# Two parts of P times V in the two banks of one tile, maxima passes six steps ahead, and outputs ahead of a new down pair: an attention and GEGLU kernel

## The chip, the cores and the metric

The kernel runs on one core of a Trainium2 chip. The metric is device microseconds (us) of one execution, the median over several runs; lower is better. The profile comes from one further execution that the hardware profiler recorded. PE is the matrix engine (TensorE), PEld its weight loads, DVE is VectorE, ACT is ScalarE, POOL is GpSimd, SP is the engine that issues most DMAs.

## The reference

A layer norm of x (2048 rows of 576) feeds two branches, and the result joins them. `wqkv`, `wo` and the three GEGLU weights are random; every product below is computed to float32 accuracy, which the kernel reaches by splitting operands into a high and a low float16 half and adding up three products.

```python
def _A_ref(x, wqkv, wo):            # S = 2048, D = 576, H = 32, Dh = 18
    qkv = (lambda x, *d: x.transpose(*d))((x @ wqkv).reshape(B, S, 3, H, Dh), 2, 0, 3, 1, 4)
    q, k, v = qkv[0], qkv[1], qkv[2]
    scores = jnp.einsum("bhqd,bhkd->bhqk", q, k) * (Dh ** -0.5)
    p = _softmax(scores, axis=-1)
    o = jnp.einsum("bhqk,bhkd->bhqd", p, v)
    return (lambda x, *d: x.transpose(*d))(o, 0, 2, 1, 3).reshape(B, S, D) @ wo
def _B_ref(x, w_gate, w_up, w_down):            # 576 -> 4608 -> 576
    h = _gelu(jnp.einsum("bsd,df->bsf", x, w_gate)) * jnp.einsum("bsd,df->bsf", x, w_up)
    return jnp.einsum("bsf,fd->bsd", h, w_down)
xn = _layernorm(x, axis=-1)
return x + _A_ref(xn, wqkv, wo) * _silu(_B_ref(xn, w_gate, w_up, w_down))
```

## The kernel before

**The work and its order.** The 32 heads go in 16 pairs. A main loop runs over the pairs p and, in each, over 64 steps i (lines 1696 to 1807). A step takes one block of scores of the pair, 128 keys by 512 queries for both heads (`qk2`, matmuls at L1402), turns it into exponentials P on ACT (L1408, or two calls L1410 and L1411 where the heads have different scales), and adds one block of an earlier pass over the scores of a later pair (`qk1`, matmuls at L1348), of which DVE takes the row maxima (L1351). Steps 0 to 31 are one half of the pair's queries, steps 32 to 63 the other. Between these stand the matmuls of the GEGLU branch: slots of gate and up products (`g_run`, matmuls at L496), down stages (`DownPair.run`, L758), and in the last pair slots of the output product with `wo` (`out_run`, L939). All of a core's PE instructions go in one order, fixed when the program is built; a planner (`make_plan`) spreads slots and stages over the steps by estimated costs, and `subtick` lets queued work of the other engines (loading and splitting weights, norms) into their own orders.

**P times V.** Every two steps give one unit (one block of 128 keys for a half's queries), and units wait in `pend`. `flush` takes them out and calls `burst`: for each unit eight passes on PE (four matmuls of float32, two passes each, 4 at a time side by side, L1427) add into one PSUM bank, and DVE then copies (L1433, at a half's start) or adds (L1435) that bank into the sum `osb`. A burst covers units of one half only. Where `pend` holds the end of one half and the start of the next, `flush` makes two parts of it, each with its own tile and its own add.

**PSUM.** `s1` and `s2` have two banks each for scores. `ma` and `mb` have one bank each; gate and up slots write them, and ACT empties them at the end of a unit of slots (L661 for gate into `gs`, L672 for up into `gv`; early in the run L542 and DVE L547 for the rest of q and k). `md` is a tile of two banks: a pair of down stages writes both and DVE adds them to `y` (L778). `MTile` (line 182) hands out `ma`, `mb` and `md` in program order, and a writer waits by semaphore until the tile's readers are through. A burst of one part takes `md`. A burst of two parts takes `ma` for the first and `md` for the second, or `ma` and `mb` where a down stage stands in that step and holds `md`.

**Maxima.** The passes `qk1` run AHEAD = 8 steps ahead of their pair: step i of pair p does block i + 8 of pair p + 1 or, from step 56, block i - 56 of pair p + 2. `max_end` closes a pair's maxima in three moves, at steps 55, 58 and 61: a last reduce on DVE (L1363) and three POOL operations (L1364 to L1366), a transpose on DVE (L1370) with a write to memory by SP (L1372), and two reads by SP (L1377) that put the maxima as two more rows into `QT`, from which the first `qk2` of that pair reads them. Queries and keys of pair p + 2 are loaded by SP at step 44 (`load_qk`). Ahead of the main loop, a prologue loop runs AHEAD + 1 steps of one `qk1` of pair 1 and 14 slots of gate and up.

**The last pair.** There is no gate and up stream any more. A step of the last pair does a down stage if one is open or can be opened, and then slots of the output product (L939), which `OutPair` puts into `ma` and `mb` or, when wide, into `md`; DVE (L979, L972) empties them into `ob`.

Of the kernel before, what the change touches and what calls it, by code (L numbers as in the profile page):

```python
# [12 lines left out]
F32 = mybir.dt.float32  # L13
# [3 lines left out]
ALU = mybir.AluOpType  # L17
# [3 lines left out]
P = 128  # L21
NT = S // P
NB = S // 512
NPAIR = H // 2
# [70 lines left out]
def kernel(ctx: ExitStack, tc: tile.TileContext, x, wqkv, wo, w_gate, w_up, w_down, out):  # L95
    nc = tc.nc
# [78 lines left out]
    def until(cond):  # L175
        while not cond():
            assert defer.items or bg
            subtick()
# [911 lines left out]
    def use(tag):  # L1090
        blocks[0] += 1
        return tag
# [226 lines left out]
            subtick()  # L1319


    AHEAD = 8
    QT, KT, VT, PM = {}, {}, {}, {}

    def load_qk(p):
# [17 lines left out]
    def qk1(p, item):  # L1343
        qt, kb = divmod(item, 4)
        s1 = ps.tile([P, 2, 512], F32, tag=use(("s1", "s2")[item % 2 if p == 0 or item < AHEAD and p == 1 else 0]), name=f"s1_{p}_{item}")
        for h in range(2):
# [67 lines left out]
    final_norm = deque()  # L1414
    osum = {}

    def burst(todo, tag):

        p, qh, k0, _, _ = todo[0]
        k1 = todo[-1][2]  # L1420
        t = MTile(tag, [P, 512], F32, 1)
        for _, _, kt, pa, pb in todo:
            for b, pt in enumerate((pa, pb)):
                for h in range(2):
                    qd = 64 * b + 32 * h
                    c0 = 38 * kt + 19 * h
                    nc.tensor.matmul(  # L1427
                        t.t[qd:qd + 32, :], VT[p][:, c0:c0 + 32], pt[:, h],
                        start=kt == k0, stop=kt == k1, skip_group_check=True,
                    )  # L1430
        if k0 == 0:
            osum[p, qh] = ap.tile([P, 512], F32, tag="osb", name=f"osb_{p}_{qh}", bufs=2)
            nc.vector.tensor_copy(osum[p, qh], t.t)  # L1433
        else:
            nc.vector.tensor_tensor(osum[p, qh], t.t, osum[p, qh], op=ALU.add)  # L1435
        t.done()
        if k1 == NT - 1:
            norm(p, qh)
# [119 lines left out]
    items = iter(range(64))  # L1558
    for k in range(AHEAD + 1):
        if k in (0, 2, 4):  # L1560
# [8 lines left out]
    pend = []  # L1569
    dn = None  # L1570
# [79 lines left out]

    def flush(tags):

        for tag in tags:
            if not pend:
                return
            n = next((k + 1 for k, u in enumerate(pend) if u[2] == NT - 1), len(pend))
            burst(pend[:n], tag)
            del pend[:n]

    units = deque([*range(8, NT), *range(8)])  # L1660
    tail = W()
# [33 lines left out]
    for p in range(NPAIR):  # L1695
        if p not in VT:
            load_v(p)
        more = p + 1 < NPAIR
        for i in range(4 * NT):
            s, half = divmod(i, 2)  # L1700
            qh, kt = divmod(s, NT)
            if p == NPAIR - 2:
                qh = 1 - qh
            if i == 0:
                until(lambda: mdone.get(p))
            if i == 44 and p + 2 < NPAIR:
                load_qk(p + 2)
            kp = p + 1 if i < 64 - AHEAD else p + 2
            if i == 64 - AHEAD:
                items = iter(range(64))  # L1710
            pt = qk2(p, 2 * qh + half, kt, "s2" if more else ("s1", "s2")[i % 2])
            if half == 0:
                pa = pt
            else:
                pend.append((p, qh, kt, pa, pt))
            if kp < NPAIR:
                qk1(kp, next(items))
            if i == 61 and more:
                steps[2]()
            now = 64 * p + i  # L1720
            held = 2 * len(pend) + (half == 0)
            if not more and i == 32:
                tail.keep = KEEP_END
            if gs.left == 0 and gs.pair is None and not gs.closed and not plan:
                load_ohl(OUT_ORDER[0])
                u = tail.unit
                late = False
                d = dn is not None or (
                    len(dnq) > 1 and held < 5 and (u is None or not u.wide)
                )  # L1730
                if d:
                    if dn is None:
                        dn = DownPair()
                    late = dn.run()
                run = pend and dn is None and (held >= 6 or kt == NT - 1 and half == 1 and i < 63)
                run = run or held >= 8
                subtick(dict(FREE, T=2.0) if not more else {"A": 0.75, "V": 0.75, "T": 2.0})
                if late:
                    dn.evac()
                    dn = None  # L1740
                if run:
                    wide = u.wide if u is not None else not tail.wide
                    flush(("ma", "mb") if dn is not None or wide else ("md", "md"))
                else:
                    if gq and i % 2:
                        for fn in gq.popleft():
                            fn()
                    if final_norm:
                        final_norm.popleft()()
                    if d or more:  # L1750
                        out_run(5 if d else 10)
                    else:
                        n = 28 * max(0, len(units) - tail.keep) + (28 if tail.unit is not None else 0)
                        credit = min(credit + min(9, n / (0.75 * (32 - i % 32))), 18)
                        while credit >= 4:
                            u = tail.unit
                            r = 14 if u is None else (u.slots - u.k) or 14
                            n = r if r <= 10 or credit >= r else (r + 1) // 2
                            n0 = tail.slots
                            out_run(n)  # L1760
                            credit -= tail.slots - n0
                            if tail.unit is not None or tail.slots == n0:
                                break
            else:
                if not plan and gs.pair is None and not gs.closed:
                    plan.extend(make_plan(now, held, dn is not None, len(dnq) // 2))
                step = plan.popleft() if plan else None
                late = False
                if step is None:
                    d = dn is not None or len(dnq) > 1 and held < 6  # L1770
                else:
                    d = step[0]
                behind = d and summed and not gs.closed
                summed = False
                if d:
                    dleft[0] -= 1
                if d and not behind:
                    if dn is None:
                        dn = DownPair()
                    late = dn.run()  # L1780
                if gs.closed:
                    gs.closed = False
                    if late:
                        dn.evac()
                        dn = None
                    subtick({"A": 2.2, "V": 0.8 if late else 2.2 if now < 256 else 1.5, "T": 0.7 + 0.86 * len(pend) + 0.73 * d}, 6)
                    two = any(u[2] == NT - 1 for u in pend[:-1])
                    flush(("ma", "mb") if d else ("ma", "md") if two else ("md", "ma"))
                    summed = not d
                else:  # L1790
                    quick = late or step is not None and step[2] < 1.45 and len(bg) < 70
                    subtick({
                        "A": 0.75, "V": 0.25 if quick else 0.75,
                        "T": 2.0 if step is None else 0.45 + step[2],
                    })
                    if late:
                        dn.evac()
                        dn = None
                    g_run(7 if step is None else step[1] or 0)
                    if behind:  # L1800
                        dn = DownPair()
                        dn.run()
            if more and i == 58:
                steps[1]()
            if more and i == 55:
                steps = max_end(p + 1)
                steps[0]()
    assert dn is None
# [5 lines left out]
        final_norm.popleft()()  # L1814
    u = tail.unit
    wide = u.wide if u is not None else not tail.wide
    flush(("ma", "mb") if wide else ("md", "md"))
    tail.keep = 0

    while final_norm:  # L1820
# [8 lines left out]
    for st in units:  # L1829
        u = OutPair(st, tail.wide)  # L1830
# [5 lines left out]
    for k, u in enumerate(stages):  # L1836
        sums = final_out(k) if k < 4 else None
# [38 lines left out]
```

## Time and profile before

| | |
|---|---|
| median of 3 runs | 2566.24 us (2565.88 to 2567.41) |
| the profiled execution | 2566.02 us, of which the span of the trace is 2563.9 us |
| PE busy, share of the span | 2494.2 us, 97% |
| DVE | 1843.1 us, 72% |
| ACT | 1657.5 us, 65% |
| POOL | 1550.5 us, 60% |
| mean granted clock of PE | 0.996 |

The execution's own time is 2.1 us longer than the span of its trace. In the rows of the profile, an instruction's group reads: line, engine, operation, output tile and input tiles, shape, count, then busy time, the mean of one in ns, and the idle time before it with what ended it. In a timeline, the first number is the start in us, the second how long the group of equal instructions lasted from the first start to the last end, and square brackets give the idle time ahead of it and what released it.

### The profile page before, as it was taken

To read this page: it belongs to the slowest core of one execution; us is meant where nothing else is said; L and a number is where in the kernel's file an instruction comes from. 1 tells how busy PE (TensorE), PEld (TensorE's weight loads), DVE (VectorE), ACT (ScalarE), POOL (GpSimd) and SP (SyncE) were. 2 spreads that over 40 slices of the span, in tenths; PEclk is the share of its full clock that TensorE was granted. 3 is DMA by queue.
4 is the path that set the end of the run, shared out by engine and by line. 5 is a ranking of instruction groups with operands and counts; after the bars stand their busy time and mean duration, and the time that the engine had idled before them with its cause. 6 is when DMAs were issued, how large, how long until landed. Compare 5 with 4: busy or idle time off the path is not lost.

```text
span 2563.9 us, 60635 instructions
## 1 busy us (share of the span) xinstructions
PE 2494.2 (97%) x25800; PEld 1314.3 (51%) x25800; DVE 1843.1 (72%) x2114; ACT 1657.5 (65%) x2066; POOL 1550.5 (60%) x1593
## 2 busy tenths in 40 slices
PE   7898999999999999999999999999999999999998
PEld 6554445455554545445454454555555545545555
DVE  7676778777776778777777777776777767677534
ACT  6125666766767666767666666677766666666664
POOL 4347664666638554758667676757576676757513
PEclk9999999999999999999999999999999999999999
DMA  4430112101130012201020111101011101100124
GB/s 154 134 103 13 31 39 80 38 19 52 31 86 20 24 41 65 46 23 52 14 52 11 38 30 40 51 15 52 16 34 30 40 22 41 45 13 14 38 63 139
DMA packets 139686, 118.66 MB, mean 46 GB/s; under 512 B 64810, under 2 KB 118832, under 8 KB 139417
## 3 DMA queue, kind: packets, MB, share of 16 engines
q1 hardware_dynamic: 136553, 106.92, 15.5%
q8 instruction: 203, 3.33, 0.6%
q0 software_dynamic: 1568, 5.37, 0.6%
q10 hardware_dynamic: 1296, 2.51, 0.3%
q14 instruction: 66, 0.54, 0.1%
HBM read 84.89 MB, written 29.61 MB: 45 GB/s over the span
## 4 chain that ended last, share of the span: by engine, by line
PE 85%; DVE 5%; ACT 3%; DMA 3%; POOL 2%; issue 2%; SPq 1%; ACTq 0%; POOLq 0%; DVEq 0%
PE mb_t L496 17%; PE ma_t L496 16%; PE md_t L758 16%; PE md_t L1427 12%; PE s L1402 9%; PE s L1348 8%; PE ma_t L1427 5%; DVE PM L1351 2%; ACT P L1408 1%; PE md_t L939 1%; DMA mxd_j<-mx_j 1%; PE pv_t L515 1%; ACT gs L661 1%; PE mb_t L1427 0%; PE mc_t L515 0%
## 5 line engine op out<-in xcount | busy, mean ns | idle before, releaser
L1351 DVE TENSOR_REDUCE PM<-s 128x2 f32<-128x1024 f32 x1024 | 1250.6, 1224 | 397.3 <-PE s L1348 387.0
L1408 ACT ACTIVATE P<-s,etab 128x1024 f32<-128x1024 f32 x896 | 996.0, 1113 | 600.9 <-PE s L1402 594.1
L496 PE MATMUL ma_t<-XHT,whi_c 64*128 64x512 f16 x1440 | 542.2, 377 | 7.6 <-ACT gs L661 3.9
L496 PE MATMUL mb_t<-XHT,whi_c 64*128 64x512 f16 x1440 | 542.1, 376 | 2.8 <-ACT gv L672 2.5
L496 PE MATMUL ma_t<-XHT,wlo_c 64*128 64x512 f16 x1296 | 487.7, 376 | 0.0
L496 PE MATMUL mb_t<-XHT,wlo_c 64*128 64x512 f16 x1152 | 433.6, 376 | 0.0
L496 PE MATMUL ma_t<-XL,whi_c 64*128 64x512 f16 x1152 | 433.5, 376 | 0.0
L496 PE MATMUL mb_t<-XL,whi_c 64*128 64x512 f16 x1152 | 433.4, 376 | 0.0
L1402 PE MATMUL s<-QT,KT 56*128 56x512 f16 x2048 | 408.4, 379 | 4.1 <-DVE PM L1351 1.3
L1348 PE MATMUL s<-KT,QT 54*128 54x512 f16 x2048 | 401.6, 377 | 5.2 <-DVE PM L1351 3.0
L496 PEld LDWEIGHTS <-whi_c 64*128 64x128 f16 x5184 | 279.2, 94 | 245.3 <-issue 23.1
L758 PE MATMUL md_t<-dhi_c,hhi 64*128 64x288 f16 x2304 | 349.3, 283 | 2.0 <-DVE y L778 1.2
L758 PE MATMUL md_t<-dhi_c,hlo 64*128 64x288 f16 x2304 | 349.0, 282 | 0.0
L758 PE MATMUL md_t<-dlo_c,hhi 64*128 64x288 f16 x2304 | 348.5, 282 | 0.0
L1427 PE MATMUL md_t<-P,VT 128*32 128x512 f32 x2872 | 334.4, 596 | 0.0
L758 PEld LDWEIGHTS <-hhi 64*128 64x128 f16 x4608 | 251.5, 94 | 136.2 <-issue 15.0
L697 POOL TENSOR_SCALAR tw<-tw 128x512 f32<-128x512 f32 x144 | 90.7, 630 | 317.4 <-ACT tw L690 316.3
L719 POOL TENSOR_TENSOR hlo<-gv,hhi 128x512 f16<-128x512 f32 x144 | 167.6, 1164 | 186.6 <-ACT hhi L712 182.8
L1402 PEld LDWEIGHTS <-KT 56*128 56x128 f16 x2048 | 124.9, 94 | 237.4 <-issue 153.4
L684 POOL TENSOR_TENSOR tw<-gs 128x512 f32<-128x512 f32 x144 | 150.8, 1047 | 145.7 <-ACT gs L661 145.2
L778 DVE SCALAR_TENSOR_TENSOR y<-md_t,c_c,y 128x576 f32<-128x576 f32 x272 | 219.2, 806 | 15.7 <-PE md_t L758 15.6
L496 PEld LDWEIGHTS <-wlo_c 64*128 64x128 f16 x2592 | 141.8, 94 | 118.0 <-issue 1.3
(264 smaller groups left out, 3943.6 us busy)
## 6 DMA issues: line engine op xcount, KB each, us to landing
draw_c<-in_B_w_down SPq DMA_DIRECT2D x18, 576.0 KB
raw_c<-in_B_w_gate SPq DMA_DIRECT2D x18, 512.0 KB
raw_c<-in_B_w_up SPq DMA_DIRECT2D x18, 512.0 KB
obr<-rd SPq DMA_DIRECT2D x30, 256.0 KB
KT<-KD SPq DMA_DIRECT2D x32, 224.0 KB
QT<-QD SPq DMA_DIRECT2D x32, 216.0 KB
VS<-vst POOLq DMA_DIRECT2D x16, 304.0 KB, 2.6
VT<-VS SPq DMA_DIRECT2D x16, 304.0 KB
```

Source lines behind the costliest of these rows:

```text
L496: m = nc.tensor.matmul(o, lw, xx, start=self.stage == 0 and self.k == 0, stop=self.stage == 1 and self.k == self.slots - 1, skip_group_che ...
L515: nc.tensor.matmul(o, xx(t), ww[:, t, i, :], start=(k == 0), stop=False)
L684: gp.tensor_tensor(st["t"], st["g"], st["g"], op=ALU.mult)
L697: gp.tensor_scalar(st["t"], st["t"], 1.0, 1.0, op0=ALU.mult, op1=ALU.add)
L719: gp.tensor_tensor(hs.lo[:, ft], st["v"], hs.hi[:, ft], op=ALU.subtract)
L758: m = nc.tensor.matmul(self.t.t[:, hf, 0:288], a[r, ft, sl], b[r, ft, 288 * hf:288 * hf + 288], start=self.stage == 0 and k == 0, stop=sel ...
L778: nc.vector.scalar_tensor_tensor(yy, y, w.c, yy, op0=ALU.mult, op1=ALU.add)
L1348: nc.tensor.matmul(s1[:, h], QT[p][r, P * qt:P * qt + P], KT[p][r, 512 * kb:512 * kb + 512], start=True, stop=True)
L1351: nc.vector.tensor_reduce(PM[p][:, :, qt, kb:kb + 1], s1, op=ALU.max, axis=AX.X)
L1402: nc.tensor.matmul(s2[:, h], KT[p][r, P * kt:P * kt + P], QT[p][r, 512 * qb:512 * qb + 512], start=True, stop=True)
L1408: nc.scalar.activation(pt, s2, AF.Exp, scale=ETAB[j0])
L1427: nc.tensor.matmul(t.t[qd:qd + 32, :], VT[p][:, c0:c0 + 32], pt[:, h], start=kt == k0, stop=kt == k1, skip_group_check=True,)
```

## The change

Three edits. (1) AHEAD goes from 8 to 6, and with it the places of the three moves of `max_end` (steps 57, 60, 62 in place of 55, 58, 61) and of `load_qk` (step 48 in place of 44). The prologue runs 7 steps in place of 9. (2) Where a burst has two parts and no down stage stands in the step, both parts go into the two banks of one `md` tile, each with its own add; it was `ma` and `md`. A burst of one part still takes `md`. (3) In the last pair, in a step in which a down pair is opened, its first stage comes behind the slots of the output product instead of ahead of them.

```diff
-    AHEAD = 8
+    AHEAD = 6
-    def burst(todo, tag):
+    def burst(todo, tag, both=None, bank=0):
-        t = MTile(tag, [P, 512], F32, 1)
+        t = MTile(tag, [P, 512], F32, 1) if both is None else both
+        sums = t.t if both is None else t.t[:, bank]
...
-                        t.t[qd:qd + 32, :], VT[p][:, c0:c0 + 32], pt[:, h],
+                        sums[qd:qd + 32, :], VT[p][:, c0:c0 + 32], pt[:, h],
...
-            nc.vector.tensor_tensor(osum[p, qh], t.t, osum[p, qh], op=ALU.add)
+            nc.vector.tensor_tensor(osum[p, qh], sums, osum[p, qh], op=ALU.add)
...
     def flush(tags):
-        for tag in tags:
-            if not pend:
-                return
+        parts = []
+        while pend:
             n = next((k + 1 for k, u in enumerate(pend) if u[2] == NT - 1), len(pend))
-            burst(pend[:n], tag)
+            parts.append(pend[:n])
             del pend[:n]
+        if len(parts) == 2 and "md" in tags:
+            both = MTile("md", [P, 2, 512], F32, 2)
+            for bank, part in enumerate(parts):
+                burst(part, "md", both, bank)
+        else:
+            for part, tag in zip(parts, tags):
+                burst(part, tag)
...
-            if i == 44 and p + 2 < NPAIR:
+            if i == 48 and p + 2 < NPAIR:
...
-            if i == 61 and more:
+            if i == 62 and more:
                 steps[2]()
...
-                if d:
-                    if dn is None:
-                        dn = DownPair()
+                new = d and dn is None
+                if new:
+                    dn = DownPair()
+                elif d:
                     late = dn.run()
...
+                if new:
+                    dn.run()
...
-                    two = any(u[2] == NT - 1 for u in pend[:-1])
-                    flush(("ma", "mb") if d else ("ma", "md") if two else ("md", "ma"))
+                    flush(("ma", "mb") if d else ("md",))
...
-            if more and i == 58:
+            if more and i == 60:
-            if more and i == 55:
+            if more and i == 57:
```

**A burst of two parts on PE.** In the kernel before this is the burst in pair 8 that ends its first half (queries 0 and 1, the names `P_0_..` and `P_1_..`) and starts its second (`P_2_..`, `P_3_..`). `s_8_..` are scores of `qk2`, `s_9_..` scores for the maxima of pair 9; "x2" stands for the two heads, and a bracket for the semaphores that a row waits for.

```order
L1348 MATMUL s_9_43_20600<-KT_18758,QT_18757 128x512
L1427 MATMUL ma_t<-P_0_14_20393,VT_19448 32x512 [waits Activation_49]
L1427 MATMUL ma_t<-P_0_14_20393,VT_19448 32x512
L1427 MATMUL ma_t<-P_1_14_20420,VT_19448 32x512 x2
L1427 MATMUL ma_t<-P_0_15_20455,VT_19448 32x512 x2
L1427 MATMUL ma_t<-P_1_15_20486,VT_19448 32x512 x2
L1427 MATMUL md_t<-P_2_0_20515,VT_19448 32x512 x2
L1427 MATMUL md_t<-P_3_0_20548,VT_19448 32x512 x2
```

The same burst in the changed kernel, where L1428 is the line of `burst`'s matmul.

```order
L1348 MATMUL s_9_42_20600<-KT_18837,QT_18836 128x512
L1428 MATMUL md_t<-P_0_15_20401,VT_19398 32x512 x2
L1428 MATMUL md_t<-P_1_15_20428,VT_19398 32x512 x2
L1428 MATMUL md_t<-P_2_0_20466,VT_19398 32x512 [waits DVE_49]
L1428 MATMUL md_t<-P_2_0_20466,VT_19398 32x512
L1428 MATMUL md_t<-P_3_0_20501,VT_19398 32x512 x2
```

The wait for ACT at the head of the first part (its tile `ma` has to be empty) is gone, and the first matmul of the second part has a wait for DVE that it did not have. There are 21 bursts of two parts in the kernel before, 14 in `ma` and `md` and 7 in `ma` and `mb`; there are 22 in the changed kernel, 18 in the two banks of one `md` and 4 in `ma` and `mb`. Which halves' ends fall into such a burst, and how many units each part has, moved a little too.

What DVE has in its order at that place in the changed kernel, from weights being prepared (`m_c`, `mx_c`) to the two sums:

```order
L267 TENSOR_REDUCE m_c_20177<-draw_c_19956 128x1
L276 TENSOR_REDUCE mx_c_20608<-m_c_20177 128x1
L279 TENSOR_REDUCE mx_c_20608<-m_c_20177 128x1
L1436 TENSOR_TENSOR osb_0_19597<-md_t,osb_0_19597 128x512
L1434 COPY osb_1_20627<-md_t 128x512
```

Both sums stand behind the row maxima of the same step and behind this preparation, as the sums of the kernel before did behind theirs.

**The start of the main loop on PE.** In the changed kernel the first `qk2` (`s_0_0_0`) follows the `qk1` block 5 of pair 1, and gate and up slots come behind.

```order
L1348 MATMUL s_1_5_2558<-KT_1429,QT_1428 128x512
L1402 LDWEIGHTS KT_1099 [waits DMAHW2_49]
L1402 MATMUL s_0_0_0_2576<-QT_1098,KT_1099 128x512 [waits DVE_49]
L1402 LDWEIGHTS KT_1099
L1402 MATMUL s_0_0_0_2576<-QT_1098,KT_1099 128x512 [waits DMAHW3_49]
```

Before, two more groups of slots and two more blocks of `qk1` stood between block 5 and `s_0_0_0`.

More of the change, by code (lines that the diff above doesn't have):

```diff
@@ L1432, in burst @@
             osum[p, qh] = ap.tile([P, 512], F32, tag="osb", name=f"osb_{p}_{qh}", bufs=2)
-            nc.vector.tensor_copy(osum[p, qh], t.t)
+            nc.vector.tensor_copy(osum[p, qh], sums)
         else:
-            nc.vector.tensor_tensor(osum[p, qh], t.t, osum[p, qh], op=ALU.add)
+            nc.vector.tensor_tensor(osum[p, qh], sums, osum[p, qh], op=ALU.add)
         t.done()
@@ L1742 @@
                     wide = u.wide if u is not None else not tail.wide
-                    flush(("ma", "mb") if dn is not None or wide else ("md", "md"))
+                    flush(("ma", "mb") if dn is not None or wide else ("md",))
                 else:
@@ L1816 @@
     wide = u.wide if u is not None else not tail.wide
-    flush(("ma", "mb") if wide else ("md", "md"))
+    flush(("ma", "mb") if wide else ("md",))
     tail.keep = 0
```

## The prediction

> **What bounds the kernel now.** I read the page first, then the busy time of the engines by stretch, then what PE waits for, and last the timeline at the places that the change touches.
>
> ```profile
> span 2563.9 us, 60635 instructions
> PE 2494.2 (97%) x25800; PEld 1314.3 (51%) x25800; DVE 1843.1 (72%) x2114; ACT 1657.5 (65%) x2066; POOL 1550.5 (60%) x1593
> ...
> PE 85%; DVE 5%; ACT 3%; DMA 3%; POOL 2%; issue 2%; SPq 1%; ACTq 0%; POOLq 0%; DVEq 0%
> ```
>
> ```profile
> 400.00:800.00 400.00, 393.36 (x3958) 202.20 (x3958) 302.45 (x342) 280.25 (x378) 235.02 (x246) 1.00 0.19 50
> 800.00:1600.00 800.00, 794.01 (x8191) 397.17 (x8185) 599.09 (x656) 535.97 (x618) 514.01 (x521) 1.00 0.14 36
> 1600.00:2400.00 800.00, 797.20 (x8324) 412.44 (x8321) 588.65 (x632) 548.66 (x686) 540.44 (x542) 1.00 0.12 30
> 2400.00:2500.00 100.00, 91.84 (x1083) 53.12 (x1080) 38.16 (x57) 67.31 (x75) 27.55 (x27) 0.98 0.21 62
> ```
>
> The rows give stretch, length, then busy time of PE, PEld, DVE, ACT and POOL, and the clock. From 400 to 2400 us PE is busy for 1984.6 of 2000 us. All PE work stands in one order, so the program is as long as that order: a wait that goes from it shortens the run by about its length, and a wait that comes in lengthens it, because next to no slack is there to soak it up. No edit changes how many products are formed. So I count waits on PE.
>
> ```profile
> PE ma_t L1427 <- ACT gs L661: 4.8, 12, 0.4
> PE ma_t L496 <- ACT gs L661: 3.9, 3, 2.6
> PE mb_t L496 <- ACT gv L672: 2.5, 3, 2.1
> PE ma_t L496 <- DVE osb L1435: 2.2, 4, 0.9
> PE ma_t L1427 <- DVE evl L547: 2.0, 2, 1.0
> PE s L1402 <- DVE PM L1351: 1.3, 1, 1.3
> ```
>
> (Sum in us, times, longest.)
>
> **Edit 2, what goes.** The 14 bursts in `ma` and `md` begin on a bank that still has to be emptied. Rows 1 and 5 are these 14 waits. One of them, on PE:
>
> ```profile
> 1466.09 0.40 PE L1348 MATMUL s<-KT,QT 54*128 54x512 f16 x2
> 1466.88 1.92 PE L1427 MATMUL ma_t<-P,VT 128*32 128x512 f32 x16 [0.40 <-ACT gs L661]
> 1468.63 1.90 PE L1427 MATMUL md_t<-P,VT 128*32 128x512 f32 x16
> ```
>
> and a burst of one part, in `md`:
>
> ```profile
> 1570.09 0.38 PE L1348 MATMUL s<-KT,QT 54*128 54x512 f16 x2
> 1570.40 2.78 PE L1427 MATMUL md_t<-P,VT 128*32 128x512 f32 x24
> ```
>
> From the maxima's matmul to the burst it takes 0.79 us in the first and 0.31 in the second: 0.48 saved, 12 times, 5.8 us; the two behind `evl` 2.0 more. One further wait is a slot that finds `ma` held by a first part's sum:
>
> ```profile
> 736.15 0.37 PE L496 MATMUL ma_t<-XHT,whi_c 64*128 64x512 f16 x1 [0.78 <-DVE osb L1435]
> ```
>
> Together 5.8 + 2.0 + 0.8 = **8.6 us saved**.
>
> **Edit 2, what comes.** In the changed order the first matmul of a second part waits for DVE. The count it waits for is reached by the sum of the first part of the same burst, in each of the 18 merged bursts: the two parts share a tile, and bank 1 isn't begun before DVE has read bank 0. Before, the second part ran on at once (1466.88 + 4 x 0.43 = 1468.60, begun at 1468.63). Behind the waiting matmul stand the rest of the burst and everything else on PE. The price is the time from the last four matmuls of part one to the end of its sum. The trace has such a wait in the last pair, where a down stage wants the bank that a burst has just filled:
>
> ```profile
> 2451.09 1.47 PE L1427 MATMUL md_t<-P,VT 128*32 128x512 f32 x12
> ...
> 2452.63 0.69 DVE L1435 TENSOR_TENSOR osb<-md_t,osb 128x512 f32<-128x512 f32 x1 [3.43 <-PE md_t L1427]
> ...
> 2453.37 0.30 PE L758 MATMUL md_t<-dhi_c,hhi 64*128 64x288 f16 x2 [0.49 <-DVE osb L1435]
> ```
>
> Four matmuls run side by side and start 0.43 us after the four ahead (24 in 2.78, 16 in 1.92: two groups more in 0.86). The last four of the 12 start at 2451.95; the sum starts 0.68 later, and PE goes on 0.74 after that: 1.42 us in place of 0.43, **0.99 lost**. That is with DVE idle (3.43 us ahead). In the main loop it isn't:
>
> ```profile
> 1466.52 1.23 DVE L1351 TENSOR_REDUCE PM<-s 128x2 f32<-128x1024 f32 x1
> 1467.66 0.68 DVE L262 TENSOR_REDUCE m_c<-raw_c 128x1 f32<-128x512 f32 x1
> 1468.25 0.74 DVE L267 TENSOR_REDUCE m_c<-draw_c 128x1 f32<-128x576 f32 x1
> 1468.91 0.68 DVE L1435 TENSOR_TENSOR osb<-ma_t,osb 128x512 f32<-128x512 f32 x1
> 1470.59 0.69 DVE L1433 COPY osb<-md_t 128x512 f32<-128x512 f32 x1 [1.00 <-PE md_t L1427]
> ```
>
> The row maxima of the step start 0.43 after their matmul (1466.09) and hold DVE to 1.57 after it; preparation of weights may follow, 0.59 for L262, 0.66 for L267, and only then the sum. A part of one unit starts 0.31 after the same matmul and has two groups, so part two would start at 0.31 + 0.86 = 1.17. With the sum at 1.57, PE goes on at 1.57 + 0.74 = 2.31: 1.14 lost, and more by what DVE has in between. From two units on the sum is ready after the maxima are done, and 0.99 stands. The order of the changed kernel gives:
> - 7 bursts with two or three units in part one: 7 x 0.99 = 6.9 us;
> - 5 with one unit and nothing between: 5 x 1.14 = 5.7;
> - 6 with one unit and preparation between. The rows for the two kinds that the timeline above doesn't show:
>
> ```profile
> L262 DVE TENSOR_REDUCE m_j<-raw_j 128x1 f32<-128x252 f32 (+1 forms) x20 | 6.7, 374 | 0.0
> L547 DVE SCALAR_TENSOR_TENSOR evl<-mb_t,evh 126x512 f16<-126x512 f32 (+1 forms) x17 | 11.6, 680 | 0.0
> L276 DVE TENSOR_REDUCE mx_c<-m_c 128x1 f32<-128x5 f32 x18 | 2.7, 147 | 0.0
> ```
>
> Back to back each takes 0.08 less than its duration (L262: 0.68 against 0.59). So three short L262, 1.0; one L547, 0.6; L267 with L276 and its like L279, 0.66 + 0.14 = 0.8, twice; L547 with two L262, 1.8; two L262, 1.2. That is 6 x 1.14 + 6.2 = 13.0 us.
>
> Sum **25.6 us lost** on 18 bursts. The bounds are 18 x 0.99 = 17.8, if DVE finds its preparation done early, and some 30, if the maxima themselves start late. What is late next is small: the sum of part two (a copy at a half's start) comes 1 to 3 us later, with the next step's maxima behind it on a DVE that is 74% busy here.
>
> The rule that speaks for the change is in the Trainium skill, PSUM — Partial Sum Buffer, "PSUM bank collisions raise a hardware error": guard by bank and quadrant, since a read of one bank and a write to another run clean. By it the wait on bank 0's reader isn't needed and this term would be 0. The trace agrees as far as banks go (the sum of `ma` at 1468.91 runs beside matmuls into `md`), but the wait is in the order, and PE obeys it whether or not the memory needs it.
>
> **The clock.** Idle stretches cost more than themselves if they slow the clock.
>
> ```profile
> 1018.00:1021.40 3.40, 2.12 (x16) 0.67 (x14) 3.40 (x6) 2.23 (x2) 0.00 (x0) 1.00 0.24 74
> ...
> 2442.80:2446.20 3.40, 1.77 (x23) 1.29 (x24) 1.67 (x4) 1.61 (x2) 0.06 (x1) 1.00 0.26 87
> 2446.20:2449.60 3.40, 3.40 (x27) 2.37 (x26) 0.82 (x1) 1.11 (x1) 1.34 (x1) 0.50 0.70 225
> ```
>
> 1.28 us idle in 3.4 left the clock at 1.00; 1.63 idle was followed by 3.4 us at 0.50, which is 1.7 us of lost work. A burst's idle time is its loss less 0.2 (the last four take 0.63, not 0.43). The six of the third kind idle 1.5 to 2.7 us; five are above 1.63, some of them cut by the edge of a stretch. I take three drops, **5.1 us**; bounds 0 and 6 x 1.7 = 10.2.
>
> The Trainium skill (TensorE: Matmul & The Clock Gate, "Why this matters for your kernels") asks for no idle gaps over about 3 us between bursts of matmuls. By that none of these stalls would slow the clock and the sum would be 5.1 us lower. The row at 2446.20 speaks against it.
>
> **Edit 1.** In the prologue the first `qk2` waited 1.3 us for DVE (row 6 of the waits). Now it comes right behind block 5 of the maxima, where PE next waits 2.6 and 2.1 us for ACT to empty `ma` and `mb` anyway (the longest of rows 2 and 3), so the wait falls into those: **-1.3 us**, bounds -3 and 0. The moves of the maxima have two steps less from the transpose to their reader:
>
> ```profile
> 349.74 0.23 DVE L1370 STREAM_TRANSPOSE rms<-rmc 128x64 f16<-128x64 f16 x1
> ...
> 350.00 0.34 SPq L1372 DMA_DIRECT2D md<-rms  x1
> ...
> 351.44 1.32 SPq L1377 DMA_DIRECT2D QT<-md  x2
> ...
> 361.44 0.38 PE L1402 MATMUL s<-QT,KT 56*128 56x512 f16 x2
> ```
>
> The two reads are out at 352.76, 3.0 us after the transpose, and have to land, which I estimate at no more than the 1.44 from write to read; 11.7 us are there. Two steps of about 2.3 us (the span less the first 200 us, over 1024 steps) leave 7 here and, by the order, 4 to 5 at the boundaries with the fewest slots. I put 0.5 us on it; bounds 0 and 1 us at each of 14 boundaries.
>
> **Edit 3.** Five steps swap a first down stage and outputs. At one, outputs now wait for a sum that the stage covered; at another, a stage no longer fills the wait for `ob`:
>
> ```profile
> 2425.50 0.69 DVE L1435 TENSOR_TENSOR osb<-ma_t,osb 128x512 f32<-128x512 f32 x1 [2.78 <-PE ma_t L1427]
> ...
> 2425.59 0.29 PE L758 MATMUL md_t<-dhi_c,hhi 64*128 64x288 f16 x2
> ```
>
> Outputs into `ma` could start at 2426.2 in place of 2425.6, +0.6, and a stage is 0.73 (2425.59 to the outputs at 2426.33), +0.7. Against that the wait of 0.49 at 2453.37 is covered, and one like it of about 0.3. Sum **+0.5**, bounds -1 and 1.5.
>
> **Sum.** 2566.0 (the profiled execution, 0.2 us under the median of 2566.24) - 8.6 + 25.6 + 5.1 - 1.3 + 0.5 + 0.5 = 2587.8, and with the 0.2 to the median **2588 us**, 22 us slower.
>
> **Rivals.**
> - *The saving as meant.* The second part's wait is met when PE gets there, because DVE runs ahead or the wait is for an older instruction. Then 2566.2 - 8.6 - 1.3 + 0.5 = 2557, faster. For it: DVE is 26% idle. Against it: the sum can't start before part one's last matmuls are done, 0.68 after they start, and lasts 0.69. It decides where a wait is below 8.6/18 = 0.48 us, and the nearest row has 0.99. Chance 0.07; another 0.05 for a wait about halfway that leaves the time within 0.2%, 5 us, which is about what a measurement of this kernel can tell from no change.
> - *The floor.* 0.99 at each burst, nothing queued ahead on DVE, no clock drop: 2566.2 - 8.6 + 17.8 - 1.3 + 0.5 = 2575. Chance 0.18.
> - *Maxima late.* The 14 boundaries lose 1 to 2 us each on top of the forecast: 2602 to 2616. For it: with weights being loaded, SP has other transfers between write and reads. Against it: 4 to 5 us of margin are about what is needed. Chance 0.10.
>
> The forecast has 0.60, by itself 2578 to 2600. The range 2572 to 2602 takes in the floor and leaves out the saving, the halfway case and most of the late maxima. Faster 0.07, same 0.06, slower 0.87.
>
> **What would show it.** In the profile after, the waits of PE should have a row of `md_t` at `burst`'s matmul behind `osb`, 18 times, in all 15 to 25 us, longest near 2.7, and rows 1 and 5 should be gone or below 1 us. Busy PE stays at 2494 but for 3 to 10 us at half clock. It is wrong if that row is absent or below 9 us, or if the new time sits at the boundaries of pairs, behind `QT`.

## The result and the profile after

| | before | changed |
|---|---|---|
| median of 5 runs | 2566.24 us (2564.02 to 2567.62) | 2588.6 us (2584.49 to 2589.99) |
| profiled execution | 2566.02 us, span 2563.9 | 2589.99 us, span 2588.2 |

The ratio is 1.0086, 95% interval 1.0072 to 1.01: 22.4 us slower (18 to 26 by the interval), where 21.8 had been forecast. The profiled execution of the changed kernel is 1.4 us above its median.

From the page of the changed kernel, and then the busy time by stretch (PE first, the clock third from the end):

```profile
span 2588.2 us, 60632 instructions
...
PE 2501.7 (97%) x25800; PEld 1296.6 (50%) x25800; DVE 1848.9 (71%) x2116; ACT 1655.6 (64%) x2066; POOL 1546.3 (60%) x1593
```

```profile
400.00:800.00 400.00, 390.46 (x3886) 197.76 (x3884) 299.66 (x335) 276.48 (x372) 226.64 (x235) 1.00 0.20 50
800.00:1600.00 800.00, 786.40 (x8120) 389.37 (x8118) 594.87 (x649) 528.29 (x611) 514.61 (x527) 1.00 0.14 36
1600.00:2400.00 800.00, 792.25 (x8280) 401.35 (x8276) 583.36 (x629) 543.09 (x681) 534.81 (x537) 1.00 0.12 30
```

PE is busy 7.5 us longer on the same 25800 instructions (3 to 10 had been forecast, for stretches at half clock), and from 400 to 2400 us it is idle for 30.9 us where it was idle for 15.4. The waits of PE say on what:

```profile
PE md_t L1428 <- DVE osb L1436: 23.7, 18, 3.5
...
PE s L1348 <- DVE PM L1351: 5.2, 7, 1.3
PE ma_t L939 <- DVE ob L979: 4.7, 2, 2.5
PE mb_t L496 <- ACT gv L672: 2.7, 3, 2.2
...
PE s L1402 <- DVE PM L1351: 1.7, 1, 1.7
...
PE ma_t L496 <- ACT gs L661: 1.5, 3, 0.6
```

The first row wasn't there before: 18 waits of a burst's matmuls for a sum, 23.7 us in all, the longest 3.5 where about 2.7 had been expected. The rows of `ma_t` at the burst's matmul behind `gs` and `evl`, 6.8 us together before, are gone. The place in pair 8 that the order showed, on PE and on DVE:

```profile
1482.68 0.38 PE L1348 MATMUL s<-KT,QT 54*128 54x512 f16 x2
1482.98 1.07 PE L1428 MATMUL md_t<-P,VT 128*32 128x512 f32 x8
1485.82 1.92 PE L1428 MATMUL md_t<-P,VT 128*32 128x512 f32 x16 [1.77 <-DVE osb L1436]
```

```profile
1483.10 1.23 DVE L1351 TENSOR_REDUCE PM<-s 128x2 f32<-128x1024 f32 x1
1484.24 0.74 DVE L267 TENSOR_REDUCE m_c<-draw_c 128x1 f32<-128x576 f32 x1
1484.90 0.15 DVE L276 TENSOR_REDUCE mx_c<-m_c 128x1 f32<-128x5 f32 x1
1485.02 0.15 DVE L279 TENSOR_REDUCE mx_c<-m_c 128x1 f32<-128x2 f32 x1
1485.09 0.68 DVE L1436 TENSOR_TENSOR osb<-md_t,osb 128x512 f32<-128x512 f32 x1
```

Part one (8 passes from 1482.98) is over at 1484.05. Its sum waits for the maxima and for L267, L276 and L279, and runs from 1485.09. Part two, which writes the other bank, begins at 1485.82. Without the wait it would have begun some 0.89 after part one, as it does in x1 below (parts at 1615.79 and 1616.68), at 1483.87, so 1.95 us went; 1.94 was the estimate for a burst with these three in DVE's queue.

### The profile page after: what moved, and what is told of

The parts are those of the page before. It is cut to its first block, busy times and chain, and to the rows that moved or that the text cites. A ratio compares the mean times of both kernels' runs of the same rounds, so it can differ in the third digit from the quotient of the medians.

```text
span 2588.2 us, 60632 instructions
## 1 busy us (share of the span) xinstructions
PE 2501.7 (97%) x25800; PEld 1296.6 (50%) x25800; DVE 1848.9 (71%) x2116; ACT 1655.6 (64%) x2066; POOL 1546.3 (60%) x1593
## 4 chain that ended last, share of the span: by engine, by line
PE 87%; DVE 6%; ACT 2%; issue 2%; POOL 2%; DMA 1%; SPq 0%; ACTq 0%; DVEq 0%; POOLq 0%
PE mb_t L496 17%; PE ma_t L496 16%; PE md_t L758 16%; PE md_t L1428 12%; PE s L1402 9%; PE s L1348 8%; PE ma_t L1428 4%; DVE PM L1351 2%; DVE osb L1436 1%; ACT P L1408 1%; PE md_t L939 1%; PE pv_t L515 1%; PE mc_t L515 0%; DVE xt L1192 0%; PE mb_t L939 0%
## 5 line engine op out<-in xcount | busy, mean ns | idle before, releaser
L496 PEld LDWEIGHTS <-whi_c 64*128 64x128 f16 x5184 | 272.8, 94 | 244.0 <-issue 16.9
L1428 PE MATMUL md_t<-P,VT 128*32 128x512 f32 x3000 | 356.0, 603 | 23.8 <-DVE osb L1436 23.7
L758 PE MATMUL md_t<-dhi_c,hhi 64*128 64x288 f16 x2304 | 343.3, 283 | 2.0 <-DVE y L778 1.7
L758 PE MATMUL md_t<-dhi_c,hlo 64*128 64x288 f16 x2304 | 342.8, 283 | 0.0
L758 PE MATMUL md_t<-dlo_c,hhi 64*128 64x288 f16 x2304 | 342.5, 282 | 0.0
L758 PEld LDWEIGHTS <-hhi 64*128 64x128 f16 x4608 | 244.4, 94 | 140.6 <-issue 12.2
L1428 PEld LDWEIGHTS md_t<-P,VT 128*32 128x32 f32 x3000 | 87.2, 110 | 231.2 <-issue 169.9
```

What stands on the lines that cost most here:

```text
L496: m = nc.tensor.matmul(o, lw, xx, start=self.stage == 0 and self.k == 0, stop=self.stage == 1 and self.k == self.slots - 1, skip_group_che ...
L758: m = nc.tensor.matmul(self.t.t[:, hf, 0:288], a[r, ft, sl], b[r, ft, 288 * hf:288 * hf + 288], start=self.stage == 0 and k == 0, stop=sel ...
L1428: nc.tensor.matmul(sums[qd:qd + 32, :], VT[p][:, c0:c0 + 32], pt[:, h], start=kt == k0, stop=kt == k1, skip_group_check=True,)
```

## The experiments

All times are medians, beside runs of the kernel before on the same chip (2564 to 2566 us).

| run | what it is | us | ratio to before, 95% |
|---|---|---|---|
| x1 | changed kernel without edit 2 | 2568.34 | 1.0013 (1.0004 to 1.0022) |
| x2 | kernel before with edit 2 alone | 2579.05 | 1.005 (1.0038 to 1.0063) |
| x3 | changed kernel, both sums behind both parts | 2566.19 | 1.0002 (0.9993 to 1.0011) |
| x4 | changed kernel, DVE's preparation behind the sums | 2587.63 | 1.0083 (1.007 to 1.0097) |
| x5 | changed kernel, a second reader of part one | 2599.22 | 1.0135 (1.0121 to 1.0149) |
| x6 | kernel before with edit 1 alone | 2563.99 | 1.0 (0.9991 to 1.0009) |
| x7 | kernel before with edit 3 alone | 2568.0 | 1.0013 (1.0004 to 1.0022) |
| x8 | kernel before, two parts in `md` then `ma` | 2567.07 | 1.0008 (0.9999 to 1.0016) |
| x9 | edit 1, `md`'s banks as two tiles, a part in each | 2565.15 | 0.9999 (0.9991 to 1.0008) |
| x10 | control for x9, parts in `ma` and `md` | 2573.67 | 1.0032 (1.0019 to 1.0044) |
| x11 | x3 with the last pair's order as before | 2564.74 | 0.9998 (0.9989 to 1.0007) |

**Is it edit 2?** x1 takes it out of the changed kernel.

```diff
-                    flush(("ma", "mb") if d else ("md",))
+                    two = any(u[2] == NT - 1 for u in pend[:-1])
+                    flush(("ma", "mb") if d else ("ma", "md") if two else ("md", "ma"))
```

with `flush` and `burst` as in the kernel before.

> The changed kernel with edit 2 alone undone: parts of a two-part burst in ma and md again, the steps of the maxima and the order in the last pair as changed. Theory (the second part's wait for the first part's sum is the loss): that wait is gone, a burst waits for ACT to empty ma again; 18 such bursts at 0.48 us where the kernel before had 14, so within some 3 us of the kernel before, 2563 to 2569 us. Rival (the maxima six steps ahead, or the last pair's order, cost the time): stays above 2578 us.

x2 puts it alone into the kernel before, the same lines the other way round.

> The kernel before with edit 2 alone: both parts in one md tile, maxima eight steps ahead, last pair as before. 14 merged bursts, 7 with one unit in part one. Theory: 7 x 0.99 + 7 x 1.14 = 14.9 us, some 5 for what DVE has queued, 5 for the clock, less 8.6 saved: 2578 to 2588 us, and a row of waits of md_t for osb with 14 entries. Rival: at or below 2566 us.

2568.3 and 2579.1: both as the theory had it. Without edit 2 all but some 3 us are gone (edit 3, below, costs about as much by itself); with it alone, on 14 bursts in place of 18, 14 us are there, at the low end of what was expected. Its row of waits has 14 entries:

```profile
PE md_t L1428 <- DVE osb L1436: 17.6, 14, 3.2
```

x1 and the changed kernel have the same bursts, so their steps can be set side by side. From one step's first `qk2` to the next, in us, worked out from the two traces, at five of the 18:

```
start in x1 / changed   x1     changed  more   units in part one; DVE between maxima and sum
 363.08 /  366.33       3.72   4.38     0.65   1; nothing
 500.27 /  507.27       3.73   4.28     0.55   2; nothing
1467.58 / 1482.46       3.72   5.22     1.50   1; L267, L276, L279
1688.55 / 1706.16       3.72   5.56     1.84   1; two L262
 289.20 /  289.20       3.72   6.99     3.27   1; three short L262, and half clock from 292.8
```

1.14 - 0.48 = 0.66 and 0.99 - 0.48 = 0.51 are what the sum gives for the first two: both terms of edit 2, the wait and the saving at the head, are there burst by burst at their estimated size.

**Is it the sum between the parts?** x3 changes only where the sums are issued.

```diff
-            for bank, part in enumerate(parts):
-                burst(part, "md", both, bank)
+            adds = [burst(part, "md", both, bank) for bank, part in enumerate(parts)]
+            for add in adds:
+                add()
```

(`burst` returns its sum as a function instead of issuing it.)

> The changed kernel with one thing altered: the matmuls of both parts are issued first, then both sums, so that no sum stands between the parts. The products, the two banks and all else stay. Theory: the 18 waits of 23.7 us go, and the clock's drops with them, and the waits for ACT to empty ma are gone too: 2553 to 2561 us, faster than both kernels. Rival (the loss lies in PE and DVE meeting in one tile, or in the other two edits): above 2575 us.

2566.2 us. The 18 waits are gone and 22.4 us with them, but the kernel isn't faster than before, which the theory had expected by 5 to 13 us. The trace shows why, in pair 9:

```profile
1616.96 0.38 PE L1348 MATMUL s<-KT,QT 54*128 54x512 f16 x2
1617.27 2.78 PE L1428 MATMUL md_t<-P,VT 128*32 128x512 f32 x24
...
1622.60 0.39 PE L1348 MATMUL s<-KT,QT 54*128 54x512 f16 x2 [0.27 <-DVE PM L1351]
```

```profile
1620.12 0.69 DVE L1437 TENSOR_TENSOR osb<-md_t,osb 128x512 f32<-128x512 f32 x1 [1.51 <-PE md_t L1428]
1620.73 0.68 DVE L1435 COPY osb<-md_t 128x512 f32<-128x512 f32 x1
1621.33 1.22 DVE L1351 TENSOR_REDUCE PM<-s 128x2 f32<-128x1024 f32 x1
```

The burst starts 0.31 after the maxima's matmul and runs through, 0.48 saved against x1. But two sums in a row now stand ahead of the next step's maxima, and two steps on, the matmul that needs the bank of those maxima waits: that step takes 2.38 where x1 takes 1.95. Of 0.48, 0.43 is given back. By steps, x3 gains 0.48 at most of the 18 bursts and pays 0.3 to 0.6 in the steps behind each of 17 of them. Behind the other, near 1028 us, it pays 3.3 in two steps: PE waits 2.1 us for the maxima there, and a stretch at half clock follows.

x11 is x3 without edit 3.

```diff
-                new = d and dn is None
-                if new:
-                    dn = DownPair()
-                elif d:
+                if d:
+                    if dn is None:
+                        dn = DownPair()
                     late = dn.run()
...
-                if new:
-                    dn.run()
```

> The best of what was seen: the changed kernel with the sums behind both parts (as x3) and the last pair's order as before. x3 was 2566.2 us and edit 3 alone cost some 1 to 3: 2562 to 2565 us, a little under the kernel before, by less than can be told apart surely. Rival (what the late sums give back grows): 2566 us or more.

2564.7, within what was expected; it can't be told from the kernel before.

**Does the place of the first sum decide?** x8 keeps two tiles and turns them round.

```diff
-                    flush(("ma", "mb") if d else ("ma", "md") if two else ("md", "ma"))
+                    flush(("ma", "mb") if d else ("md", "ma"))
```

> The kernel before with its 14 two-part bursts in md and then ma, two tiles as before but the other way round: no wait for ACT at the burst's head, 14 x 0.48 = 6.7 us saved there, and part two's sum on ma comes after the last matmul, where the next step's slots want ma: their first may start 0.68 + 0.69 + 0.05 after the burst's last four instead of 0.43 + 0.43, some 0.6 us lost each time. Theory (what is saved at the head comes back at the next user of the tile): 2563 to 2571 us. Rival (the saving stands): below 2560 us.

2567.1, as the theory had it. At most of its 14 bursts the step is 0.48 shorter and the next one 0.43 longer, behind the sum on `ma`, which the kernel before had beside the matmuls of part two. At one, near 735 us, the slot waits 2.3 us for that sum and a stretch at half clock follows. The common case:

```profile
1472.77 0.69 DVE L1433 COPY osb<-ma_t 128x512 f32<-128x512 f32 x1 [0.52 <-PE ma_t L1427]
```

```profile
1473.52 0.37 PE L496 MATMUL ma_t<-XHT,whi_c 64*128 64x512 f16 x1 [0.27 <-DVE osb L1433]
```

x9 has both at once: the banks of `md` shared, and the first sum beside part two. `md` becomes two tiles of one bank.

```diff
-                self.t = MTile("md", [P, 2, 512], F32, 1)
+                self.t = [MTile(tag, [P, 512], F32, 1) for tag in ("md", "me")]
...
-            y = self.t.t[:, :, 0:288]
+            for hf, t in enumerate(self.t):
+                y = t.t[:, 0:288]
...
-                    flush(("ma", "mb") if d else ("ma", "md") if two else ("md", "ma"))
+                    flush(("ma", "mb") if d else ("md", "me"))
```

> The kernel before with the maxima six steps ahead (edit 1), the two banks of md as two tiles of one bank each, and the parts of a two-part burst in these two. A pair of down stages takes both tiles, and its evacuation is two operations on DVE in place of one. So the banks are shared as edit 2 wanted, without the wait for part one's sum, and with that sum beside part two's matmuls. Theory (the loss is the tile's wait alone, the saving at the head of 18 bursts stands when the first sum isn't late): 8.6 us below the control x10, which is at 2564 to 2572 us: 2555 to 2564 us. Rival (what is saved at the head comes back a step later, as with the sums last): within 3 us of the control.

The wide outputs of the last pair take the two tiles too. The control x10 is the same without the last of these edits.

> Control for x9: maxima six steps ahead and md as two tiles of one bank, two operations to empty a down pair, but two-part bursts in ma and md as in the kernel before. It prices the second operation: by the rows of the outputs' evacuation (two of 0.51 us, 0.43 apart, 0.94 against 0.81 for one) 288 x 0.13 = 37 us more of DVE work, most of it beside PE: 2564 to 2572 us under every theory.

x9 is 8.5 us below x10, where 8.6 had been expected; both are 1 to 2 us above the upper end of what was expected for them by themselves. In x9 the sum starts beside part two, and at this burst and most others nothing is given back:

```profile
1617.02 0.68 DVE L1429 TENSOR_TENSOR osb<-md_t,osb 128x512 f32<-128x512 f32 x1
1618.61 0.69 DVE L1427 COPY osb<-me_t 128x512 f32<-128x512 f32 x1 [0.91 <-PE me_t L1421]
1619.22 1.22 DVE L1345 TENSOR_REDUCE PM<-s 128x2 f32<-128x1024 f32 x1
```

The exception is again near 1026 us, where PE waits for late maxima and a stretch at half clock follows, which x10 doesn't have:

```profile
1026.02 0.39 PE L1342 MATMUL s<-KT,QT 54*128 54x512 f16 x2 [2.06 <-DVE PM L1345]
```

By steps, the two traces differ by 11.0 us saved and 3.3 given back, most of it there; that the medians are 8.5 apart, so near 8.6, is in part luck. So two banks can be shared at no wait, and most of the saving that edit 2 aims at is there. It doesn't pay here, since a down pair's evacuation in two operations costs some 8 to 10 us (x10 against x6: 9.7 by the medians, 8.4 in the main loop of the two traces). The two rows in x9, for one of 806 ns in the kernel before:

```profile
L779 DVE SCALAR_TENSOR_TENSOR y<-me_t,c_c,y 128x288 f32<-128x288 f32 x272 | 138.1, 508 | 0.0
L779 DVE SCALAR_TENSOR_TENSOR y<-md_t,c_c,y 128x288 f32<-128x288 f32 x272 | 137.7, 506 | 13.8 <-PE md_t L758 13.8
```

**Is the wait paid one to one?** x5 adds a reader of part one's bank in each merged burst; its result is used by nothing.

```diff
             nc.vector.tensor_tensor(osum[p, qh], sums, osum[p, qh], op=ALU.add)
+            if both is not None and bank == 0:
+                twice = sm.tile([P, 1], F32, tag="twice", name=f"twice_{p}_{qh}", bufs=1)
+                nc.vector.tensor_reduce(twice, sums, op=ALU.max, axis=AX.X)
```

> The changed kernel with one more reader of part one in each of the 18 merged bursts: after its sum, DVE takes a maximum over the same bank into a spare column that nothing uses. Theory (PE's order has no slack, so the wait on part one's readers goes into the time one to one): 18 x 0.66 = 11.9 us more of waits, and up to 6 for further stretches at half clock: 2600 to 2608 us. Rival (part of the wait is soaked up further on, as the moved preparation came back further on): below 2595 us.

2599.2, 10.6 more than the changed kernel, and 0.8 under the expected range.

```profile
PE md_t L1428 <- DVE twice L1439: 34.4, 18, 4.1
```

The waits grow by 10.7 us, 0.60 in each burst and not 0.66 (back to back the second reader ends 0.60 after the first), and the time grows by as much.

**What DVE has queued.** x4 puts the preparation behind the sums.

```diff
+                    two = not d and any(u[2] == NT - 1 for u in pend[:-1])
+                    if not two:
+                        subtick(room, 6)
                     flush(("ma", "mb") if d else ("md",))
+                    if two:
+                        subtick(room, 6)
```

> The changed kernel with the preparation of weights that DVE had ahead of a merged burst's sums put behind them, in all 18 bursts; each still has its wait. Theory with DVE's queue and the clock as terms: 7 x 0.99 + 11 x 1.11 = 19.1 us of waits in place of 26.9, and no stretch at half clock between 230 and 2400 us, since no burst idles over 1 us: 2572 to 2578 us. Rival (the wait costs the same whatever DVE has queued, and the half clock is no part of it): 2585 to 2590 us.

2587.6 us: the theory failed on the time. The waits at the bursts shrink, by 6.3 of the 7.8 us that it said (two bursts still wait 1.7, behind `evl`), and there is no half clock between 230 and 2400 us, but another wait doubles:

```profile
PE md_t L1428 <- DVE osb L1436: 17.4, 18, 1.7
PE s L1348 <- DVE PM L1351: 10.2, 15, 1.3
...
PE mb_t L496 <- DVE evl L547: 1.8, 4, 0.7
```

That is 6.3 us less at the sums, 5.0 more at the maxima and 1.4 more at `evl` (0.4 in the changed kernel). The same place in pair 8:

```profile
1485.66 0.69 DVE L1434 COPY osb<-md_t 128x512 f32<-128x512 f32 x1 [2.05 <-PE md_t L1428]
1486.27 0.74 DVE L267 TENSOR_REDUCE m_c<-draw_c 128x1 f32<-128x576 f32 x1
...
1487.12 1.22 DVE L1351 TENSOR_REDUCE PM<-s 128x2 f32<-128x1024 f32 x1
```

```profile
1488.39 0.39 PE L1348 MATMUL s<-KT,QT 54*128 54x512 f16 x2 [0.52 <-DVE PM L1351]
```

DVE stood idle for 2.05 us while part two ran, and then had the preparation still to do, ahead of the next maxima. So the waits about cancel. In the two traces the main loop, from its first exponential to its last, is 3.8 us shorter than in the changed kernel, about what the half clock is worth there (4.5, below); in the medians 1.0 us of that remains, and the start of the loop varies by some 3 us between traces (below). How much of the 1.0 each part has can't be settled from this run.

**Edits 1 and 3 alone.** x6 is the change of AHEAD and of the four step numbers, x7 the change in the last pair's block, both in the kernel before.

> The kernel before with edit 1 alone: maxima six steps ahead. 18 bursts in ma and md in place of 14, at 0.48 us each, 1.9 us; the prologue's wait gone, -1.3; the maxima in time, 0 to 1: 2564 to 2568 us. Rival (maxima late at the 14 boundaries): above 2572 us.

> The kernel before with edit 3 alone: in the last pair outputs ahead of a new down pair's first stage. By the sum +0.5 us, by the trace of the changed kernel about +1: 2565 to 2567 us. Rival (the last pair carries some of the loss of 22): above 2570 us.

x6 is 2564.0, on the low side and not to be told from no change: no boundary got late, and no `qk2` waits for `QT` in its trace. What 4 more bursts in `ma` and `md` cost and what the shorter prologue saves can't be told apart in the total. The trace shows the saving: the three waits at the start of the main loop, for `gs`, `gv` and the first `qk2`'s maxima, were 2.6, 2.1 and 1.3 us and are 0.3, 2.2 and 1.7 in x6 and in the changed kernel. The wait for the maxima is still there, and the wait for `gs` falls into it: 6.0 us before, 4.2 now.

x7 is 2568.0, 1 us above what was expected and 2 below its rival; with its interval it is 1 to 6 us slower than the kernel before. In its trace, which is of the fastest of its eleven executions, the first exponential to the last takes 0.4 us longer than before, close to the 0.5 of the forecast: steps of the last pair are 0.65 and 1.42 us longer where outputs now wait, and three others 0.59, 0.61 and 0.43 shorter. Two more pairs of runs differ by edit 3 alone, x1 and x6, x3 and x11, and in their traces the same stretch is 2.5 us longer with it. With edit 3 outputs wait for `ob` longer, here x1 and then x6:

```profile
2447.03 0.28 PE L939 MATMUL ma_t<-whi_wo,ohl 64*128 64x288 f16 x1 [2.50 <-DVE ob L979]
```

```profile
2444.57 0.28 PE L939 MATMUL ma_t<-whi_wo,ohl 64*128 64x288 f16 x1 [1.38 <-DVE ob L979]
```

A stretch at half clock follows in x1, x3 and x7, and none in x6 and x11. The profiled execution of the kernel before has one there without edit 3 (the row at 2446.20 of the prediction), as x2, x8, x9 and x10 have, which would make its difference from x7 small. How much of the 2.9 is the clock stays open.

## Why the prediction was right

Its steps, with what the runs showed (in us):

| step | forecast | shown |
|---|---|---|
| the bound: PE's order, no slack | a wait costs its length | x5: 10.7 more of waits, 10.6 more of time |
| saved at the bursts' heads | -8.6 on 14 bursts | 0.48 a burst (x3, x8, x9 against their pairs); x9 - x10 -8.5 on 18, 7.6 in the main loop of the traces |
| waits for part one's sum | 25.6, bounds 17.8 and 30 | 26.9: idle 23.7 plus 18 x 0.18 |
| half clock | 5.1, three drops | 4.5 in the main loop (steps against x1), some 1.6 in the last pair; PE busy 7.5 longer in all |
| prologue and maxima | -1.3 and +0.5 | together -1.1 with x6's interval of 2.3 to either side; the three waits at the start -1.8 |
| the last pair | +0.5 | +0.4 in the trace of x7; 2.9 by its median, 2.5 in the traces of x1 and x6: above the bound of 1.5 |

The total came within 0.6 us of the forecast. That is closer than its terms, of which the waits came out 1.3 larger, the clock about 1 and edit 3 some 2, and closer than the interval of 18 to 26 us can tell; so much closeness is luck.

**The waits** came burst by burst as the order and DVE's durations said: 0.99 for seven of them, 1.10 for five, 1.95 twice for L267 and its followers, 2.07 for the three short L262, 2.29 for the two long ones. Two were larger than their sums, 2.49 in place of 1.7 and 3.67 in place of 2.9: at both, `evl` stands ahead of the maxima too and delays them by 0.8, which the prediction gave only as a bound ("if the maxima themselves start late").

**The clock** slowed after three bursts in the main loop, as taken, though after one of them for two stretches. That it was three is in part luck, since which stall the edge of a stretch cuts was not known: the one of 2.11 us ahead of 1709.87 was cut and had no stretch at half clock behind it. In the changed kernel, stretches cut where the clock changes (busy PE first, granted clock third from the end):

```profile
289.39:292.80 3.41, 1.52 (x16) 0.28 (x16) 2.93 (x6) 2.27 (x3) 2.40 (x3) 1.00 0.00 0
292.80:296.21 3.41, 3.41 (x18) 0.49 (x17) 0.00 (x0) 0.00 (x0) 1.75 (x2) 0.50 0.03 5
439.59:443.00 3.41, 1.10 (x15) 0.17 (x10) 2.89 (x4) 1.33 (x2) 0.00 (x0) 1.00 0.71 231
443.00:446.41 3.41, 3.41 (x20) 0.77 (x14) 0.58 (x1) 0.05 (x1) 0.00 (x0) 0.50 0.41 132
958.41:961.82 3.41, 1.64 (x16) 0.31 (x15) 2.65 (x5) 1.87 (x3) 3.24 (x4) 1.00 0.02 0
961.82:965.24 3.42, 3.42 (x34) 1.26 (x28) 1.82 (x2) 1.11 (x1) 1.62 (x2) 1.00 0.17 9
1030.09:1033.50 3.41, 1.41 (x12) 0.16 (x8) 3.09 (x5) 2.08 (x3) 0.00 (x0) 1.00 0.11 29
1033.50:1036.91 3.41, 1.92 (x10) 0.26 (x12) 1.43 (x3) 0.00 (x0) 0.00 (x0) 0.50 0.13 42
1036.91:1040.33 3.42, 3.42 (x21) 1.23 (x20) 1.92 (x2) 1.11 (x1) 0.00 (x0) 0.50 0.23 65
```

1.89, 2.31 and 2.00 us idle in a stretch of 3.41 were followed by half clock; 1.77 was not. In a stretch already at half clock, 1.49 idle was followed by another. The Trainium skill's rule of no idle gaps over about 3 us (TensorE: Matmul & The Clock Gate, "Why this matters for your kernels") would have let two of the three bursts pass, with gaps of 1.89 and 2.31 us, and caught only the third, with 3.49; these rows are stricter than the rule. A gap of 2.23 us in x2 was let pass, as the rule has it (below). On the window itself the Trainium skill agrees with the rows: the same page gives 3413 ns, free-running (Part 1), and the stretches at half clock from 292.80, 443.00 and 1033.50 begin 44 and 173 times 3.413 us apart.

**The rivals.** *The saving as meant* fell, and in two ways. The wait is real (x3 against the changed kernel, 22.4 us), so the time couldn't be 2557; and where the wait is taken away by issuing the sums later (x3), the time is 2566 and not 2557, because DVE pays back most of the saving through the next maxima. Only with the first sum beside part two (x9) does the saving stay. *The floor* fell with the six bursts that wait 1.7 us and more. *Maxima late* fell with x6.

**What it had not seen.** "What is late next is small" held for the changed kernel, where the first sum is out of the way before part two ends, and not for its neighbours: in x3 and x8 the late sum returns 0.3 to 0.6 for each 0.48, and in x4 the moved preparation returns its time at the maxima. The 6.2 us that the forecast puts on DVE's queue came out at 7.8 (14.4 on the six bursts, less 6 x 1.10), but a better place for that queue can't win them back in full: DVE has to do the work somewhere between two maxima.

## What to carry to other kernels

Sharing a tile that has a bank for each of two parts isn't free when a reader of the first part stands between them in the program: the second part's first write waits for that reader, even in the other bank, and in an order without slack it pays the whole latency of a sum, here 0.99 us and whatever that engine has queued. Look in the instruction order for a new wait at the head of the second part, and price it from a place in the trace where a writer follows a reader of its own output. A saving at the head of a stage is kept only if the next user of the engines isn't handed it back: compare step by step, not only the total.

## What the runs showed of the hardware

The clock of PE halves for a whole stretch of about 3.41 us, on a fixed grid. In the changed kernel's main loop it did so after stretches in which PE was idle for 1.89 us or more, and didn't after 1.77; in the last pair of the kernel before, 1.63 was enough. Idle time alone doesn't decide, for in x2 a stretch with 2.04 us idle was followed by full clock:

```profile
445.88:449.29 3.41, 1.37 (x16) 0.42 (x16) 1.99 (x3) 0.43 (x1) 0.00 (x0) 1.00 0.63 220
449.29:452.70 3.41, 3.41 (x44) 1.76 (x38) 2.06 (x3) 1.51 (x2) 0.00 (x0) 1.00 0.41 133
```

What decides between 1.6 and 2.0 is open. Eight passes of P times V in such a stretch take 1.94 us in the changed kernel, against 1.07 at full clock:

```profile
1034.99 1.94 PE L1428 MATMUL md_t<-P,VT 128*32 128x512 f32 x8 [3.49 <-DVE osb L1436]
```

The start of the main loop moves by some 3 us between kernels whose program is the same up to there. The first exponential is at 214.83 us in x7, and in the kernel before and in x8 at:

```profile
216.09 1.11 ACT L1408 ACTIVATE P<-s,etab 128x1024 f32<-128x1024 f32 x1 [0.61 <-PE s L1402]
```

```profile
218.10 1.11 ACT L1408 ACTIVATE P<-s,etab 128x1024 f32<-128x1024 f32 x1 [0.62 <-PE s L1402]
```

So differences under 3 us are better read from the steps inside the loop than from a single execution's total.
